# The up product of twelve MLP blocks by Strassen's scheme, in two rounds

## The chip, the cores and the metric

The kernel runs on one core of a Trainium2 chip, and its time is the device time of that core in microseconds, the median of three runs. A core has five engines that work side by side, each on its own list of instructions in order: TensorE (PE, matmuls), VectorE (DVE), ScalarE (ACT), GpSimd (POOL) and SyncE (SP, which here only issues DMAs). An instruction waits until those of other engines that it names in its semaphores are through, and everything behind it on its engine waits too.

## The reference

Three parts in a row, in float32, for 8 batches of 576 tokens:

```
phi(x) = exp(+-(x @ w_phi - max|x @ w_phi|))                # 64 -> 128 features, both signs
x   = (phi(q) @ (phi(k)^T v)) / (phi(q) . sum phi(k))       # linear attention, 8 heads of 64
xn  = layernorm(x) * g
x   = x + relu(xn @ w_ch1) @ w_ch2                          # 512 -> 2048 -> 512
th  = x @ w_theta
y   = w_tok_r @ (x cos th) + w_tok_i @ (x sin th)           # 576 x 576, over tokens
u   = x + y
out = u + relu(u @ w_ch)                                    # 512 -> 512
```

## The kernel before

Every float32 product is three matmuls on numbers that are split in a high and a low part: `mm3` (L74 to L77) issues high x high, high x low and low x high. A high part is a copy by ACT (`hi_act`), a low part the difference to it by DVE (`lo_vec`, L63) or POOL (`lo_pool`, L66). The big weights arrive as 64-bit numbers. `conv64` makes float32 of them with one ACT operation (L106) and four on DVE (L107, L108, L109, L114); `split64` adds the high and low parts.

The 2048 hidden units of the MLP are 16 blocks of 128. **Stage A** (up to 686 us) is attention, LayerNorm and the first 4 blocks for chunks of 256 tokens (`mlp_a`); after attention its last chunks remain, a tail from about 612 to 686 us, beside which the weights of the other 12 blocks are converted (`mb.loads`, at the lowest priority). Stage A leaves the normalised tokens in DRAM (`xn_d`) and the partial result (`xp_d`). **Stage B** (686 to 1312 us) does the other 12 blocks: 18 chunks of 256 tokens, each in six steps of two blocks. A step is `up` (24 `ph` matmuls of 256 columns), `relu` (L174 ACT, L175 DVE, with 512 columns each), and the `down` of the step before (12 `acc` matmuls of 512 columns). After the sixth step `flush_b` adds the partial result (L614) and stores the tokens (`x2_d`). The weights of the mixing are converted by `loads_mix` beside the first chunks, low parts on DVE. **Stage C** (1312 us to the end) takes batch after batch: `prep` loads and transposes a tile of 128 tokens, `theta` multiplies by w_theta and forms cosine and sine with POOL (L717), DVE (L718 to L720, L727, L63) and ACT (L723 to L725); `mix` and `channels` are the two products that follow. For the first batch, `prep` and `theta` are called inside the last chunk of stage B.

The order of the instructions on each engine is made once, when the program is built: a scheduler takes the calls with a priority (program order, moved down by `tc.high_priority(offset=LOWP)` or up by `HIP`) and lists them by its own estimate of when each can start.

Of the kernel before, what the change touches and what calls it, by code (L numbers as in the profile page):

```python
# [20 lines left out]
P = 128  # L21
# [30 lines left out]
def body(ctx, tc, qT, kT, va, wbd, g, w1, w2, wth, wtok, wch, out):  # L52
# [77 lines left out]
    class Mlp:  # L130
        """A range of the hidden units: weights and their loads, cut in steps of two blocks of 128."""
# [46 lines left out]
    # ---- attention and the first hidden units  # L178
# [393 lines left out]
    cur = tokens_b(0)  # L572
# [34 lines left out]
    def flush_b():
        acc, f, hh, hl, ch = pend
        mb.down(f, acc, hh, hl)
        if f == NFB // 2 - 1:  # L610
            x = p_mb.tile([P, CT, DM], F32, name="x")
            SY.dma_start(out=x, in_=xp_d[ch])
            for i in range(CT):
                V.tensor_tensor(x[:, i, :], acc[i], x[:, i, :], op=ALU.add)  # L614
            SY.dma_start(out=x2_d[ch], in_=x)

    # ---- rotation and the mixing of tokens and of channels: small tiles take the places of weights that are through
    class Slots:
        """Tiles that rotate through the slots of other tiles."""

        def __init__(self, *names):
            self.names, self.n = names, 0

        def tile(self, shape, dtype):
            tag = self.names[self.n % len(self.names)]
# [297 lines left out]
```

## Time and profile before

| what | us |
| --- | --- |
| median of three runs | 1757.18 (1756.98 to 1759.02) |
| span of the profiled execution | 1755.6 |
| median less span | 1.6 |
| stage B, 108 steps | about 686 to 1312 |
| stage C | about 1312 to 1755.6 |

The span is from the first to the last instruction of one profiled execution; what lies around it is the 1.6 us. Read the busy shares by stretch, not over the whole: DVE and POOL are loaded up to 740 us and again from 1312 us, while PE is loaded all the time.

```
PE   7899999899999898999999999999999999999999
DVE  8988798987898599886112212211247656656562
POOL 6786777777776243200000000000023222322220
```

These are tenths of busy time in 40 slices of 43.9 us each, from the page's second section; stage B is the slices 16 to 30.

### The profile page before, as it was taken

What the parts mean: (1) busy time and instruction counts of PE and PEld (TensorE: products, weight loads), DVE (VectorE), ACT (ScalarE), POOL (GpSimd) and SP (SyncE); (2) the same over time, 40 slices, a digit from 0 to 9 for tenths busy, and PEclk for the clock granted to TensorE, in tenths of its full rate; (3) what the DMA queues carried; (4) which work ended last, traced back from release to release, by engine and by line L of the source; (5) the groups of instructions that cost most, each with busy time, mean ns of one, the idle gap of its engine ahead of it and who ended that gap; (6) DMA issues with size and microseconds to landing.
All of it is one profiled execution on the core that took longest, in us unless ns stands there. A gap on an engine that the chain in (4) does not pass through costs nothing.

```text
span 1755.6 us, 29078 instructions
## 1 busy us (share of the span) xinstructions
PE 1691.7 (96%) x11596; PEld 1546.8 (88%) x11596; DVE 1076.5 (61%) x1910; ACT 670.5 (38%) x1236; POOL 601.4 (34%) x544
## 2 busy tenths in 40 slices
PE   7899999899999898999999999999999999999999
PEld 5787998899899687889999998999888999999999
DVE  8988798987898599886112212211247656656562
ACT  6675666666666434343111111111133223322330
POOL 6786777777776243200000000000023222322220
PEclk9999999999999999999999999999999999999999
DMA  5334333234331366445111111111032211212101
GB/s 182 98 101 125 92 111 111 79 104 127 103 113 58 120 197 192 155 138 176 49 37 49 61 37 37 64 46 37 25 98 77 70 52 38 57 46 75 52 14 41
DMA packets 80070, 151.13 MB, mean 86 GB/s; under 512 B 7232, under 2 KB 34240, under 8 KB 79936
## 3 DMA queue, kind: packets, MB, share of 16 engines
q1 hardware_dynamic: 79936, 149.29, 27.1%
q8 instruction: 91, 1.49, 0.4%
q14 instruction: 43, 0.35, 0.1%
HBM read 95.78 MB, written 49.28 MB: 83 GB/s over the span
## 4 chain that ended last, share of the span: by engine, by line
PE 76%; DVE 14%; POOL 3%; issue 3%; ACT 2%; DMA 1%; SPq 0%; DVEq 0%; POOLq 0%; ACTq 0%
PE ph L75 6%; PE ph L76 6%; PE ph L77 6%; PE acc L77 6%; PE acc L75 6%; PE acc L76 6%; PE mx L75 4%; PE mx L76 4%; PE mx L77 4%; PE ch L77 2%; PE ch L76 2%; PE ch L75 2%; PE th L76 2%; PE th L77 2%; PE th L75 2%
## 5 line engine op out<-in xcount | busy, mean ns | idle before, releaser
L175 DVE SCALAR_TENSOR_TENSOR hl<-ph,hh 128x512 fp32r<-128x512 f32 x138 | 95.0, 688 | 362.4 <-ACT hh L174 362.2
L75 PE MATMUL ph<-xh,w 128*128 128x256 f32 x1104 | 312.7, 283 | 2.6 <-DVE xl L63 1.6
L76 PE MATMUL ph<-xl,w 128*128 128x256 f32 x1104 | 311.4, 282 | 1.7 <-DVE xl L63 1.6
L77 PE MATMUL ph<-xh,w 128*128 128x256 f32 x1104 | 310.5, 282 | 0.0
L174 ACT ACTIVATE hh<-ph 128x512 fp32r<-128x512 f32 x138 | 82.0, 596 | 436.2 <-PE ph L77 426.0
L75 PE MATMUL acc<-w,hh 128*128 128x512 f32 x576 | 229.4, 399 | 4.8 <-ACT hh L174 3.1
L77 PE MATMUL acc<-w,hl 128*128 128x512 f32 x576 | 224.8, 399 | 3.5 <-DVE hl L175 3.4
L76 PE MATMUL acc<-w,hh 128*128 128x512 f32 x576 | 228.0, 396 | 0.0
L75 PEld LDWEIGHTS ph<-xh,w 128*128 128x128 f32 x1104 | 209.1, 189 | 9.4 <-DVE xl L63 1.6
L76 PEld LDWEIGHTS ph<-xl,w 128*128 128x128 f32 x1104 | 209.3, 190 | 7.8 <-DVE xl L63 2.5
L77 PEld LDWEIGHTS ph<-xh,w 128*128 128x128 f32 x1104 | 209.2, 190 | 0.3
L737 POOL TENSOR_TENSOR xs<-xs 128x512 f32<-128x512 f32 x4 | 5.5, 1374 | 560.5 <-DVE xs L63 560.5
L75 PE MATMUL mx<-wtk,xs 128*128 128x288 f32 x576 | 171.6, 299 | 1.3 <-POOL xs L57 1.3
L76 PE MATMUL mx<-wtk,xs 128*128 128x288 f32 x576 | 169.5, 295 | 0.0
L77 PE MATMUL mx<-wtk,xs 128*128 128x288 f32 x576 | 168.2, 295 | 0.0
L77 PEld LDWEIGHTS acc<-w,hl 128*128 128x128 f32 x576 | 106.6, 188 | 28.9 <-DVE hl L175 5.9
L75 PEld LDWEIGHTS acc<-w,hh 128*128 128x128 f32 x576 | 108.6, 189 | 25.1 <-ACT hh L174 3.9
L76 PEld LDWEIGHTS acc<-w,hh 128*128 128x128 f32 x576 | 108.4, 188 | 18.8
L270 DVE TENSOR_TENSOR ys<-pj,m 128x512 f32<-128x512 f32 (+1 forms) x160 | 99.6, 626 | 34.5 <-ACT pf L280 20.6
L75 PEld LDWEIGHTS mx<-wtk,xs 128*128 128x128 f32 x576 | 109.0, 189 | 2.0 <-POOL xs L57 1.8
L76 PEld LDWEIGHTS mx<-wtk,xs 128*128 128x128 f32 x576 | 109.1, 189 | 0.1
L77 PEld LDWEIGHTS mx<-wtk,xs 128*128 128x128 f32 x576 | 108.4, 189 | 0.0
(176 smaller groups left out, 4260.3 us busy)
## 6 DMA issues: line engine op xcount, KB each, us to landing
raw<-in_w SPq DMA_DIRECT2D x32, 512.0 KB, 3.8
in<-in_va SPq DMA_DIRECT2D x30, 325.0 KB, 3.0
xd<-xo SPq DMA_DIRECT2D x48, 192.0 KB, 2.1
x<-xd SPq DMA_DIRECT2D x36, 256.0 KB, 2.8
xnd<-xt SPq DMA_DIRECT2D x18, 512.0 KB, 3.0
xpd<-x SPq DMA_DIRECT2D x36, 256.0 KB, 2.9
xt<-xnd SPq DMA_DIRECT2D x18, 512.0 KB, 3.5
x<-xpd SPq DMA_DIRECT2D x18, 512.0 KB, 3.5
```

The source lines that it names most:

```text
L75: T.matmul(out_, lhsT=lh, rhs=rh, start=start, stop=False, **kw)
L76: T.matmul(out_, lhsT=lh, rhs=rl, start=False, stop=False, **kw)
L77: T.matmul(out_, lhsT=ll, rhs=rh, start=False, stop=stop, **kw)
L174: A.activation(hh, ph, AF.Relu)
L175: V.scalar_tensor_tensor(hl, ph, 0.0, f32(hh), op0=ALU.max, op1=ALU.subtract)
L270: V.tensor_tensor(ys[:, :2 * n, :], pv, m[:, :2 * n].unsqueeze(2).to_broadcast([P, 2 * n, NF]), op=ALU.subtract)
L737: G.tensor_tensor(x4, f32(pre[1]), f32(pre[2]), op=ALU.add)
```

## The change

Stage B works on 9 chunks of 512 tokens, in **two rounds** of three pairs of hidden blocks (54 steps, class `Hidden`). The up product of a pair is a 2 x 2 product of blocks: two halves of the 512 tokens by two halves of the 512 inputs (`a11`, `a12`, `a21`, `a22`), by two halves of the inputs by two hidden blocks. It is formed in seven parts instead of eight, in Winograd's form of Strassen's scheme, with four sums of token blocks (`s1` to `s4`, on POOL) and four of weight blocks (`tw`, on POOL). Each part is 6 matmuls of 256 columns (`part`), so a pair takes 42 instead of 48; results are combined on the way out of PSUM: some parts accumulate in one PSUM tile (`pa`), `keep` copies it on ACT, `plus` adds another on DVE, `relu` splits the sum (ACT and DVE, 256 columns). The down product is as before.

Round one leaves its partial sums in DRAM (`xq_d`). The weights of round two are prepared within round one (`loads_b`): two of the three pairs go to DRAM and come back by DMA at the end of the round, the third takes a free slot. The low parts of all these weights are made by POOL. The mixing weights are converted in round two (`loads_mix`), low parts on POOL; the token matrix now goes through DRAM (`wtk_d`). `prep` and `theta` of the first batch stand behind stage B.

```diff
+        def prep(self, stage, lo=lo_pool):
+            vs = stage.tile([P, KC, 2 * P], F32, name="vs")
+            for l in range(2):
+                val = self.conv(stage, w1[:, 2 * l:2 * l + 2, o:o + 2 * P], 2, 2 * P)
+                for c in range(2):
+                    A.activation(vs[:, 2 * l + c, :], val[:, c * 2 * P:(c + 1) * 2 * P], AF.Copy,
+                                 scale=gs[:, 2 * l + c:2 * l + c + 1])
+                yield
...
+            G.tensor_tensor(t[:, 0], b12, b11, op=ALU.subtract)
+            G.tensor_tensor(t[:, 2], b22, b12, op=ALU.subtract)
+            G.tensor_tensor(t[:, 1], b22, t[:, 0], op=ALU.subtract)
+            G.tensor_tensor(t[:, 3], b21, t[:, 1], op=ALU.subtract)
...
+            for d in (slice(3, 5), slice(5, 7)):
+                x = t[:, d.start - 3:d.stop - 3]
+                hi_act(h[:, d], x)
+                lo(l[:, d], x, h[:, d])
...
-        xt = p_m0.tile([P, KC, NC_], F32, name="xt")
-        SY.dma_start(out=xt, in_=xn_d[ch])
-        hi_act(xh, xt)
-        lo_vec(xl, xt, xh)
...
+        G.tensor_tensor(s1, a21, a22, op=ALU.add)
+        G.tensor_tensor(s2, s1, a11, op=ALU.subtract)
+        G.tensor_tensor(s3, a11, a21, op=ALU.subtract)
+        G.tensor_tensor(s4, a12, s2, op=ALU.subtract)
+        for n, src in (("a11", a11), ("a12", a12), ("s2", s2), ("s1", s1), ("s3", s3), ("a22", a22), ("s4", s4)):
+            h, l = (p_xb.tile([P, 2, NC_], F32R, name=n + i) for i in "hl")
+            hi_act(h, src)
+            lo_vec(l, src, h)
...
-            split64(p_st, wth[:, c, :], *wths[c])
+            split64(p_st, wth[:, c, :], wths[c][:, 0, :], wths[c][:, 1, :], pool_lo=True)
...
+        def part(self, ps, w, x, start, stop):
+            xh, xl = self.xs[x]
+            for k in range(2):
+                mm3(ps, self.q.wa[:, 0, w, k, :], self.q.wa[:, 1, w, k, :], xh[:, k, :], xl[:, k, :],
+                    start and k == 0, stop and k == 1, skip_group_check=True)
...
+        def first(self):
+            self.part(a, 0, "a11", True, True)
+            p1 = self.keep(a, "p1")
+            self.part(b, 1, "a12", True, True)
+            c11 = self.plus(b, p1, "c11")
+            self.relu(c11, 0, 0)
+            self.part(a, 4, "s2", False, True)
+            self.u2 = self.keep(a, "u2")
+            self.part(c, 3, "s1", True, True)
+            self.part(a, 5, "s3", False, True)
+            u3 = self.keep(a, "u3")
+            c22 = self.plus(c, u3, "c22")
+            self.relu(c22, 1, 1)
+        def second(self):
+            self.part(self.a, 6, "a22", False, True)
+            self.relu(self.a, 1, 0)
+            self.part(self.c, 2, "s4", False, True)
+            c12 = self.plus(self.c, self.u2, "c12")
+            self.relu(c12, 0, 1)
...
+    for r in range(2):
+        for ch in range(NCH // 2):
+            for n in range(NR):
+                hid = Hidden(slots[n], xs)
+                hid.first()
+                if pend is not None:
+                    flush_b()
+                hid.second()
+                if n == NR - 1 and not (r and last):
+                    cur = tokens_b(0 if last else ch + 1)
+                with tc.high_priority(offset=LOWP):
+                    next(gl if r == 0 else gx, None)
...
-                elif f >= 4:
-                    bs[0].theta(f - 4)
-                    bs[0].prep(f - 3)
...
+    x4, pre = shared_prep(0)
+    shared(0, pre)
+    for i in range(4):
+        bs[0].prep(i)
+        bs[0].keep(i)
+        bs[0].theta(i)
```

Three places show how the lists of instructions change. Lines are those of the kernel that the list belongs to.

PE within a step of stage B. Before, the end of an up product and what follows (`ph` is the PSUM tile of the up product, `acc` that of the down product, `w` a weight):

```order
L75 MATMUL ph<-xh,w_4_1_0_8269 128x256
L76 MATMUL ph<-xl,w_4_1_0_8269 128x256
L77 MATMUL ph<-xh,w_4_1_1_8270 128x256
L75 MATMUL acc_14205<-w_4_4_0_8281,hh 128x512 [waits Activation_49]
L76 MATMUL acc_14205<-w_4_4_1_8282,hh 128x512
L77 MATMUL acc_14205<-w_4_4_0_8281,hl 128x512 [waits DVE_49]
L75 MATMUL acc_14206<-w_4_4_0_8281,hh 128x512
```

The changed kernel, at the same place in a step (`pa`, `pb`, `pc` are PSUM tiles of the parts, `wa` and `wd` the weights of a pair):

```order
L75 MATMUL pc<-s4h,wa_8268 128x256
L76 MATMUL pc<-s4l,wa_8268 128x256
L77 MATMUL pc<-s4h,wa_8268 128x256
L75 MATMUL acc_9396<-wd_8269,hh 128x512 [waits Activation_49]
L76 MATMUL acc_9396<-wd_8269,hh 128x512
L75 MATMUL acc_9397<-wd_8269,hh 128x512
L76 MATMUL acc_9397<-wd_8269,hh 128x512
L75 MATMUL pc<-s1h,wa_8270 128x256 [waits DVE_49]
```

Before, the down product waits for one ReLU over both blocks, with the whole up product of the next step in front of it. Now `acc` takes the halves as they come, with a single part between a half's own product and its use, and the next part (`s1`) waits for DVE to have emptied `pc`.

DVE beside the conversion of weights. Before, in the first steps of stage B (`hl` is an eviction, `bits` and `val` the conversion, `xl` the tokens of the next chunk):

```order
L109 SCALAR_TENSOR_TENSOR bits<-raw,bits 128x512 [waits DVE_49]
L175 SCALAR_TENSOR_TENSOR hl<-ph,hh 128x512 [waits Activation_49]
L114 SCALAR_TENSOR_TENSOR val<-mag,bits 128x512 [waits DVE_49,Pool_49]
L175 SCALAR_TENSOR_TENSOR hl<-ph,hh 128x512 [waits Activation_49]
L63 TENSOR_TENSOR xl<-xt,xh 128x1024 [waits DMAHW2_49,Activation_49]
L107 TENSOR_SCALAR bits<-raw 128x512 [waits DMAHW0_49,DVE_49]
L175 SCALAR_TENSOR_TENSOR hl<-ph,hh 128x512 [waits PE_49,Activation_49]
```

The changed kernel, round one (`c` is a sum of parts on the way out of PSUM, `hl` the low part of its ReLU, `s3l` a token low part):

```order
L696 TENSOR_TENSOR c_9975<-pc,u_9973 128x256 [waits Activation_49]
L63 TENSOR_TENSOR s3l<-s_10026,s3h 128x512 [waits PE_49,Activation_49]
L117 SCALAR_TENSOR_TENSOR val<-mag,bits 128x512 [waits DVE_49]
L703 SCALAR_TENSOR_TENSOR hl<-c_9975,hh 128x256 [waits Activation_49]
L696 TENSOR_TENSOR c_10095<-pb,p_10087 128x256 [waits Activation_49]
L110 TENSOR_SCALAR bits<-raw 128x512 [waits DMAHW2_49,DVE_49]
L111 SCALAR_TENSOR_TENSOR bits<-raw,bits 128x512 [waits DVE_49]
L703 SCALAR_TENSOR_TENSOR hl<-c_10095,hh 128x256 [waits PE_49,Activation_49]
L112 SCALAR_TENSOR_TENSOR bits<-raw,bits 128x512 [waits DVE_49]
L703 SCALAR_TENSOR_TENSOR hl<-pa,hh 128x256 [waits Activation_49]
```

The conversion keeps its place between the evictions. There are now seven of those to a step, each half as wide, and the low parts of the weights are gone from the list.

PE at the end of stage B. Before, theta of the first batch in the last chunk (`th` theta, `tp` a transposed tile):

```order
L75 MATMUL acc_14206<-w_4_5_0_8283,hh 128x512
L76 MATMUL acc_14206<-w_4_5_1_8284,hh 128x512
L77 MATMUL acc_14206<-w_4_5_0_8283,hl 128x512
L75 MATMUL th<-wth_9472,xs 128x512 [waits Activation_49]
L76 MATMUL th<-wth_9473,xs 128x512
L77 MATMUL th<-wth_9472,xs 128x512 [waits DVE_49]
```

The changed kernel (`xs` here holds w_theta):

```order
L75 MATMUL acc_15403<-wd_12477,hh 128x512
L76 MATMUL acc_15403<-wd_12477,hh 128x512
L77 MATMUL acc_15402<-wd_12477,hl 128x512 [waits DVE_49]
L77 MATMUL acc_15403<-wd_12477,hl 128x512
L75 MATMUL th<-xs,xh 128x512 [waits Activation_49]
L76 MATMUL th<-xs,xh 128x512 [waits Pool_49]
L77 MATMUL th<-xs,xl 128x512 [waits DVE_49]
```

The last down matmuls come first now, all of theta behind them; its second and third rows wait for the low parts that POOL and DVE make.

## Rows read from the trace of the kernel before

**Rows 1.** The page, section 1: busy us (share of the span) and instructions of each engine.

```profile
PE 1691.7 (96%) x11596; PEld 1546.8 (88%) x11596; DVE 1076.5 (61%) x1910; ACT 670.5 (38%) x1236; POOL 601.4 (34%) x544
```

**Rows 2.** Stretches; columns: start:end, length, busy us (instructions) of each engine, PE's clock, DMA share, GB/s.

```profile
612.00:687.00 75.00, 68.25 (x423) 59.01 (x423) 73.73 (x101) 29.27 (x53) 28.69 (x19) 1.00 0.59 186
687.00:740.00 53.00, 48.33 (x307) 43.09 (x306) 46.71 (x62) 21.63 (x36) 13.70 (x9) 0.97 0.52 161
740.00:800.00 60.00, 60.00 (x376) 53.88 (x375) 52.66 (x117) 24.70 (x53) 0.00 (x0) 1.00 0.52 158
800.00:1200.00 400.00, 400.00 (x2547) 361.12 (x2547) 92.92 (x130) 59.57 (x94) 0.00 (x0) 1.00 0.17 56
...
1312.00:1350.00 38.00, 36.70 (x234) 33.21 (x233) 32.28 (x52) 15.39 (x28) 17.20 (x20) 1.00 0.32 110
```

**Rows 3.** PE's instructions in stage B; columns: start us, us, engine, line, operation.

```profile
901.29 0.39 PE L75 MATMUL acc<-w,hh 128*128 128x512 f32 x1
...
904.08 0.28 PE L75 MATMUL ph<-xh,w 128*128 128x256 f32 x1
...
906.95 0.39 PE L75 MATMUL acc<-w,hh 128*128 128x512 f32 x1
```

**Rows 4.** ScalarE and DVE around the same place.

```profile
901.49 0.60 ACT L174 ACTIVATE hh<-ph 128x512 fp32r<-128x512 f32 x1 [5.07 <-PE ph L77]
902.11 0.69 DVE L175 SCALAR_TENSOR_TENSOR hl<-ph,hh 128x512 fp32r<-128x512 f32 x1 [2.81 <-ACT hh L174]
```

**Rows 5.** DVE's operations by shape, 740 to 1200; after the bar busy us, mean ns.

```profile
L108 DVE SCALAR_TENSOR_TENSOR bits<-raw,bits 128x288 int32<-128x288 int32 x18 | 8.2, 455 | 0.4
...
L109 DVE SCALAR_TENSOR_TENSOR bits<-raw,bits 128x512 int32<-128x512 int32 x7 | 4.8, 687 | 0.1
...
L107 DVE TENSOR_SCALAR bits<-raw 128x512 int32<-128x512 int32 x6 | 2.6, 427 | 1.5 <-DMA raw<-in_wch 1.1 <-DMA raw<-in_wth 0.3
```

**Rows 6.** DVE's instructions at 692.

```profile
692.49 1.67 DVE L109 SCALAR_TENSOR_TENSOR bits<-raw,bits 128x512 int32<-128x512 int32 x1
```

**Rows 7.** POOL's instructions at 692.

```profile
692.01 1.60 POOL L66 TENSOR_TENSOR w<-val,w 128x512 fp32r<-128x512 f32 x1 [2.49 <-ACT w L120]
```

**Rows 8.** DVE's operations by shape, 612 to 740.

```profile
L109 DVE SCALAR_TENSOR_TENSOR bits<-raw,bits 128x512 int32<-128x512 int32 x25 | 24.7, 990 | 0.5
L108 DVE SCALAR_TENSOR_TENSOR bits<-raw,bits 128x512 int32<-128x512 int32 x26 | 23.2, 893 | 0.6
L114 DVE SCALAR_TENSOR_TENSOR val<-mag,bits 128x512 f32<-128x512 f32 x25 | 21.4, 856 | 1.3
L107 DVE TENSOR_SCALAR bits<-raw 128x512 int32<-128x512 int32 x26 | 14.8, 569 | 1.4 <-DMA raw<-in_wth 0.9
L175 DVE SCALAR_TENSOR_TENSOR hl<-ph,hh 128x512 fp32r<-128x512 f32 x13 | 8.8, 681 | 0.2 <-ACT hh L174 0.2
...
L481 DVE TENSOR_SCALAR xn<-x,lmv,lrs 128x512 f32<-128x512 f32 x8 | 6.6, 826 | 0.0
```

**Rows 9.** POOL's operations by shape, 612 to 740.

```profile
L66 POOL TENSOR_TENSOR w<-val,w 128x512 fp32r<-128x512 f32 x18 | 28.1, 1561 | 53.2 <-ACT w L120 34.2 <-ACT w L124 19.0
L489 POOL TENSOR_TENSOR xt<-xh,xl 128x512 f32<-128x512 f32 x10 | 14.4, 1445 | 33.9 <-DVE xl L63 25.5 <-PE tr L485 4.3 <-issue 3.5
```

**Rows 10.** The page, section 6: DMA issues, count, KB each, median us to landing.

```profile
xt<-xnd SPq DMA_DIRECT2D x18, 512.0 KB, 3.5
```

**Rows 11.** DVE's L720, once per tile of theta, at the start of the mixing.

```profile
1314.04 0.41 DVE L720 TENSOR_SCALAR xs<-xs 128x512 f32<-128x512 f32 x1
...
1321.72 0.43 DVE L720 TENSOR_SCALAR xs<-xs 128x512 f32<-128x512 f32 x1
```

**Rows 12.** A stretch of 2 us, columns as in rows 2.

```profile
724.00:726.00 2.00, 2.00 (x6) 1.60 (x5) 2.00 (x2) 0.47 (x2) 2.00 (x1) 0.50 0.06 16
```

**Rows 13.** PE's instructions around it; in brackets the wait and its releaser.

```profile
720.88 0.50 PE L75 MATMUL acc<-w,hh 128*128 128x512 f32 x1 [2.10 <-ACT hh L174]
...
726.08 0.36 PE L75 MATMUL ph<-xh,w 128*128 128x256 f32 x1
```

More of the change, by code (lines that the diff above doesn't have):

```diff
@@ L95, in body, with conv64 @@
     V.memset(halfpi, math.pi / 2)
-    def conv64(stage, src, pool_end):
+    def conv64(stage, src, pool_end, loaded=False):
         rows, n = src.shape
-        raw = stage.tile([rows, n], I64, name="raw", bufs=2)
-        SY.dma_start(out=raw, in_=src)
+        if loaded:
+            raw = src
+        else:
+            raw = stage.tile([rows, n], I64, name="raw", bufs=RAWB)
+            SY.dma_start(out=raw, in_=src)
         w = raw.bitcast(I32).rearrange("p (n two) -> p n two", two=2)
@@ L564, in body @@
+    NPR = NFB // 2
+    NR = NPR // 2
     s_st, p_st = opened(name="st1", bufs=1, side="right")
-    mb = Mlp(p_wb, p_st, NFA, NFB)
-    gl = mb.loads(*TAILM)
+    spare = Pair(NR + 1, NR)
+    slots = [Pair(m, m) for m in range(NR)]
+    gl = (None for q in slots for _ in q.prep(p_st))
     tail = chunk + 1
@@ new lines, in flush_b @@
+    def flush_b():
+        hid, acc, r, ch, n = pend
+        hid.down(acc, n == 0, n == NR - 1)
+        if n == NR - 1:
+            x = p_mb.tile([P, 2 * CT, DM], F32, name="x")
+            if r == 0:
+                for i in range(2):
+                    SY.dma_start(out=x[:, i * CT:(i + 1) * CT, :], in_=xp_d[2 * ch + i])
+            else:
+                SY.dma_start(out=x, in_=xq_d[ch])
+            for i in range(2 * CT):
+                V.tensor_tensor(x[:, i, :], acc[i], x[:, i, :], op=ALU.add)
+            if r == 0:
+                SY.dma_start(out=xq_d[ch], in_=x)
+            else:
+                for i in range(2):
+                    SY.dma_start(out=x2_d[2 * ch + i], in_=x[:, i * CT:(i + 1) * CT, :])
@@ new lines, in body, with loads_b @@
+    wx_d = [(dram.tile([P, 2, 7, 2, P], F32, name=f"wad{i}"), dram.tile([P, 2, 2, DM], F32, name=f"wdd{i}"))
+            for i in range(NR - 1)]
+    nxt_slots = []
+    def loads_b():
+        for i in range(NR - 1):
+            q = Pair(NR + 1 + i, NR) if i else spare
+            yield from q.prep(p_st)
+            SY.dma_start(out=wx_d[i][0], in_=f32(q.wa))
+            SY.dma_start(out=wx_d[i][1], in_=f32(q.wd))
+        q = Pair(NR, NR)
+        nxt_slots.append(q)
+        yield from q.prep(p_st)
@@ new lines, in body @@
+    flush_b()
+    for _ in gx:
+        pass
+    s_ps.close()
+    s_mb.close()
+    s_st.close()
+    s_xb.close()
+    s_p1, s_ps = ExitStack(), ExitStack()
+    ps_tr, ps_th = pool("xtp", 1, s_p1), pool("xth", 2, s_p1)
+    ps_mx, ps_ch = pool("xmx", 3), pool("xch", 2)
+    s_xc, pc = opened(name="xc", bufs=1, side="left")
+    wtks = [t[:, i] for q in slots for t in [in_slot("wa", q.slot, [3, 2, S])] for i in range(3)]
+    wtk_t = wtks
+    wchs = [t[:, i] for q in slots[:2] for t in [in_slot("wd", q.slot, [2, 2, DM])] for i in range(2)]
@@ L618, in body, with __init__, __call__ @@
+    wths = [(t[:, 0, :], t[:, 1, :]) for t in wths]
+    wtks = [(t[:, 0, :], t[:, 1, :]) for t in wtks]
+    s_xm, pm = opened(name="xm", bufs=1, side="left")
     class Slots:
[L621 to L625, printed above, removed]
+        def __init__(self, *places):
+            self.places, self.n = places, 0
+        def __call__(self, shape, dtype):
+            pl, tag = self.places[self.n % len(self.places)]
@@ L638, in body, with rot @@
+    def rot(pl, name, n):
+        return lambda shape, dtype: pl.tile(shape, dtype, name=name, bufs=n)
+    sl_z = Slots((p_wb, f"wd{slots[2].slot}"), *((pm, f"z{i}") for i in range(5)))
+    sl_x, sl_xh, sl_xl = rot(pc, "x", 3), rot(pc, "xh", 2), rot(pc, "xl", 2)
+    sl_k, sl_x4, sl_sc = rot(pc, "k", 3), rot(pc, "x4", 1), rot(pc, "sc", 4)
+    sl_cz = [rot(pm, "czh", 3), rot(pm, "czl", 3)]
     class Batch:
@@ L696, in prep @@
     def prep(p, t):
-        x = sl_x.tile([P, DM], F32)
+        x = sl_x([P, DM], F32)
         gt = p * NT + t
@@ L734, in shared_prep @@
     def shared_prep(p):
[L735 removed]
+        x4 = sl_x4([P, KC, P], F32)
         pre = prep(p, 4)
```

213 lines of the change are left out of this document (118 added, 95 removed).

## The prediction

> **What bounds the kernel now.** I read the page's busy line first: TensorE (PE) works 1691.7 us of a span of 1755.6, VectorE (DVE) 1076.5 [rows 1]. The table of stretches then says where that share is an average over two kinds of stage [rows 2]. From 612 to 740, the tail of stage A and the first steps of stage B, PE lacks 6.75 us of 75 and 4.67 of 53, and DVE is at 73.73 of 75. From 740 on PE has no gap: 60.00 of 60 while DVE still converts weights at 52.66 of 60 with GpSimd (POOL) idle, and 400.00 of 400 while DVE works 92.92. So in stage B only PE's own work sets the time, and its price can be read off the list of PE's instructions [rows 3]: 12 down matmuls of 512 columns take from 901.29 to 904.08, 2.79 us, or .2325 each; 24 up matmuls of 256 columns from 904.08 to 906.95, 2.87 us, or .1195 each; a step is 5.66. The eviction of a step is far from late: ReLU starts at 901.49 and the low part ends at 902.80 [rows 4], and its product is next needed 4 us later. A cut of PE's work in stage B is therefore worth its full length, as long as DVE and POOL keep up. That is the question here.
>
> **What the change removes.** A pair of hidden blocks over 512 tokens takes 48 up matmuls before, 42 after, all of 256 columns with a 128x128 weight as before; the down matmuls stay 24. There are 9 chunks of 512 tokens and 6 pairs, 54 in all: 54 x 6 x .1195 = -38.7 us. PE's part per pair becomes 42 x .1195 + 24 x .2325 = 10.6 us (11.3 before).
>
> **What it adds on DVE and POOL.** A conversion is four DVE operations; at 512 columns they take .43 + 3 x .69 alone [rows 5], 2.3 us from start to start with the small overlap that the rows show. Per pair, DVE gets seven evictions of 256 columns in place of two of 512 (about .35 each, an estimate at half of .69), and per chunk seven low parts of 512 (.60). That alone fits under PE. What doesn't is the neighbourhood of POOL. While a POOL subtraction runs from 692.01 to 693.61, a DVE operation on SBUF that began inside it takes 1.67 instead of .69 [rows 6, 7]. Grouped over 612 to 740: the conversion's L109, L108, L114, L107 take 990, 893, 856, 569 ns apiece, against 687 (L109, and the other two are of its kind) and 427 (L107) later, with POOL idle [rows 5, 8]. Over their 25 or 26 instructions that is 7.6 + 5.3 + 4.2 + 3.7 = 20.8 us, and 8 normalisations (L481) at 826, where an operation of this kind takes 427, add 3.2: 24 us for 28 POOL operations (18 and 10) [rows 8, 9]. So each costs DVE about .9 us. An eviction from PSUM isn't held: L175 takes 681 in the same stretch. [...]
>
> *Tail of stage A.* 12 conversions instead of 14 (-4.6 on DVE), but all 15 POOL operations of 512 and 15 of 256 of the first three pairs in place of 9 of 512: 6 x .9 + 15 x .45 = 12. DVE was at 73.73 of 75, so the 7 us more would show in full, less what the scheduler shifts: +3, bounds -5 (DVE stops being late at all, 6.75 back in part) to +7.
>
> *Start of stage B.* Nothing is left to convert there at once, but the first chunk's tokens pass a longer chain: the load xt<-xnd takes 3.5 [rows 10], then POOL makes s1 and s2 one after the other (3 us) and ScalarE and DVE split them (1.3), while PE has only the parts on a11 and a12, 1.4 us. I take about 8 us of idle, contention and slow clock against the 4.67 + .03 x 53 = 6.3 that stood there [rows 2]: +2, bounds -4 to +8.
>
> *Round one, its first seven pairs.* The order of the changed kernel has 14.7 conversions, 14 token low parts, 43 evictions and 8 sums of partial results there: 14.7 x 2.3 + 14 x .6 + 43 x .35 + 8 x .6 = 62 us of DVE, with 15 POOL operations of 512, 15 of 256 and 4 token sums: 19 x .9 + 15 x .45 = 24. That makes 86 us against 7 x 10.6 = 74 of PE, 12 too much. Since evictions from PSUM aren't held, I take 10. Bounds: 0, as in the row where 52.66 of 60 on DVE cost PE nothing, and 20, where each POOL operation holds DVE for its own 1.56.
>
> *Round two, its first eight pairs.* 18 conversions of 288 columns (.3 + 3 x .40 = 1.5 each, by the 455 ns of rows 5), 5 of 512, 18 token low parts, 57 evictions, 11 sums: 27 + 11.5 + 10.8 + 20 + 6.6 = 76. On POOL 18 low parts of 288 (at .5), 8 of 512 and about 12 token sums, of which I count 8: 9 + 14 = 23. That is 99 against 85 of PE, 14 too much; for the same reason I take 12, bounds 0 and 20.
>
> *All other pairs.* The seven evictions are in line with PE; one is tight: between the last part of a22 and the first acc matmul that needs its ReLU stand six matmuls of s4, .72 us, and ReLU needs .3 to .4 at 256 columns (half of the .60 in rows 4, plus its fixed part) and the hand-over: +2, bounds 0 to +8. Storing and reloading round two's weights and the partial sums finds the DMA engines at 17% in 800 to 1200 [rows 2]; I put that at 0, to +2.
>
> *Start of the mixing.* Before, theta of the first batch lies among the last chunk's matmuls, and PE lacks only 1.3 of 38 at 1312 [rows 2]. Now it stands behind stage B. After the last down matmul PE has five theta products of 2.8, transposes of about 2, and 7/9 of three mx groups of 27 (63 x .135 = 8.5): 24.5 us. They end on z of the fourth tile. That comes about 10 us for the first tile (theta 2.8, ScalarE, POOL, three DVE operations, sine, product, high and low part) plus four times DVE's work on a tile, nine operations or 5.1 us without POOL and 7.7 as it stands at 1314 to 1322 [rows 11]: 30 to 41, at 6.1 34.5. PE idles 10 instead of 1.3: +9, bounds +5 to +15.
>
> **Sum**, against the profiled execution: -38.7 + 3 + 2 + 10 + 12 + 2 + 9 = -0.7, a span of 1754.9. The median of the runs stands 1.6 above that span (1757.2 to 1755.6), so 1756.5 us: no change that shows. What can be told from no change is about .2%, 3.5 us.
>
> **Rivals.**
> First, DVE never gets late. For it: PE lost nothing in 740 to 800 with DVE at 88% [rows 2]; conversions are the lowest in priority. Against it: POOL was idle there, and POOL is what the change loads. Then each stretch costs 3 and the mixing 5: -38.7 + 3 + 2 + 3 + 3 + 2 + 5 = -20.7, 1736.5 us.
>
> [...]
>
> Third, the change doesn't do what it says: the seven parts, with their results evicted one by one through four PSUM tiles, never run at the pace of [rows 3]; .5 us of wait in every pair (the tight ReLU above with a late DVE) is 54 x .5 = 27, less the 2 already counted: 1781 us. Against it: the order puts 5 us of other matmuls in front of most uses.
>
> **How the numbers follow.** The forecast has .43, the first rival .29, the clock .22, the slow parts .06. The forecast's own range is 1747 to 1766, from half of the spread of its bounds; about .38 of it lies below 1753.7, .40 within 3.5 us of 1757.2, .22 above. Faster: .43 x .38 + .29 x .97 = .44. Same: .43 x .40 + .03 = .20. Slower: .43 x .22 + .22 x .95 + .06 = .36. The range that holds 8 in 10 runs from the first rival with its own spread to the second: 1733 to 1776.
>
> **What would show it.** Right: pairs of 10.6 us in the list of PE's instructions wherever no conversion stands beside them; in both conversion stretches DVE above 95% and PE with gaps that end on ACT hh, DVE hl or a DVE sum; DVE operations on SBUF of 1.3 us and more beside POOL subtractions; about 10 us of PE idle where theta starts, that ends on POOL or DVE. [...]

## The result

The changed kernel takes 1778.1 us (median of 4 runs, 1775.1 to 1779.4) against 1757.1 (1755.6 to 1759.0): ratio 1.0122, 95% interval 1.0107 to 1.0137. It is slower by 21 us, just above the range, where no change was forecast. Its profiled execution has a span of 1777.3.

The stretches of the changed kernel, with the columns of [rows 2]:

```profile
612.00:691.00 79.00, 70.54 (x414) 61.85 (x412) 70.80 (x87) 32.48 (x63) 54.68 (x40) 0.94 0.48 158
691.00:711.00 20.00, 15.98 (x84) 13.72 (x83) 14.08 (x21) 7.96 (x18) 12.11 (x8) 0.83 0.61 211
711.00:799.00 88.00, 70.20 (x402) 60.09 (x401) 85.31 (x119) 43.43 (x99) 49.64 (x38) 0.96 0.58 203
799.00:1008.00 209.00, 208.77 (x1307) 187.47 (x1307) 114.56 (x215) 78.72 (x189) 32.55 (x24) 1.00 0.35 127
1008.00:1144.00 136.00, 124.66 (x736) 108.33 (x735) 119.99 (x212) 61.60 (x151) 53.31 (x42) 0.97 0.61 204
1144.00:1305.00 161.00, 160.59 (x999) 143.82 (x998) 82.76 (x157) 56.68 (x137) 21.99 (x16) 1.00 0.33 117
1305.00:1380.00 75.00, 67.41 (x393) 58.34 (x392) 52.81 (x83) 27.58 (x50) 27.57 (x32) 0.98 0.31 98
```

A pair has 66 matmuls. From 799 to 1008 PE is full and does 1307 of them in 209 us, 10.55 us a pair: the saving is there. From 711 to 799 it does 402, or 6.1 pairs, in 88 us where 64.5 would do, and DVE is busy for 85.3 of them. From 1008 to 1144 it is 736, 11.2 pairs, in 136 where 118 would do.

To put every microsecond somewhere, I call *lost time* what has passed less what the matmuls begun until then take at full pace (.1192 for 256 columns, .2328 for 512, .1333 for 288); waits and slow clock both count. It grows as follows; the first two rows are set right under "Why the prediction was wrong".

| term | forecast | before | after | measured |
| --- | --- | --- | --- | --- |
| PE's work | -38.7 | 1717.0 | 1679.8 | -37.2 |
| lost until stage B begins | +3 | 24.8 | 28.9 | +4.1 |
| its start (before: to 740; after: one pair) | +2 | 7.2 | 8.5 | +1.3 |
| round one, pairs 2 to 7 | +10 | 0 | 23.8 | +23.8 |
| round two, pairs 1 to 11 | +12 | 0 | 17.8 | +17.8 |
| all other pairs | +2 | .4 | .8 | +.4 |
| start of the mixing, 66 us | +9 | 3.0 | 13.3 | +10.3 |
| the rest | 0 | 3.2 | 4.4 | +1.2 |
| span | -0.7 | 1755.6 | 1777.3 | +21.7 |

What PE waits for between 711 and 799 (engine, line, waited for: us in total, times, longest):

```profile
PE acc L77 <- DVE hl L703: 10.9, 5, 3.2
PE acc L75 <- ACT hh L702: 2.9, 3, 2.4
PE pb L75 <- DVE c L696: 2.2, 1, 2.2
PE pc L75 <- DVE c L696: 1.8, 1, 1.8
```

All of it is late evictions. DVE's operations there, by shape:

```profile
L111 DVE SCALAR_TENSOR_TENSOR bits<-raw,bits 128x512 int32<-128x512 int32 x14 | 17.5, 1247 | 0.3
L703 DVE SCALAR_TENSOR_TENSOR hl<-c,hh 128x256 fp32r<-128x256 f32 x18 | 13.6, 770 | 0.0
...
L110 DVE TENSOR_SCALAR bits<-raw 128x512 int32<-128x512 int32 x13 | 10.5, 805 | 0.1
...
L703 DVE SCALAR_TENSOR_TENSOR hl<-pa,hh 128x256 fp32r<-128x256 f32 x6 | 2.5, 411 | 0.0
```

The conversion is held by POOL as in [rows 8]: L111 takes 1247 ns on the mean where L109, the same kind of operation, takes 687 in [rows 5]; L110 takes 805 where L107 takes 427. Look at the two forms of L703, one and the same operation: with the sum in SBUF (`hl<-c`) it takes 770 ns, straight from PSUM (`hl<-pa`) 411. This is how one wait comes about; first DVE, then POOL, then PE:

```profile
745.20 1.77 DVE L112 SCALAR_TENSOR_TENSOR bits<-raw,bits 128x512 int32<-128x512 int32 x1
746.89 2.36 DVE L703 SCALAR_TENSOR_TENSOR hl<-c,hh 128x256 fp32r<-128x256 f32 x2
749.17 0.41 DVE L703 SCALAR_TENSOR_TENSOR hl<-pa,hh 128x256 fp32r<-128x256 f32 x1
```

```profile
745.12 2.44 POOL L66 TENSOR_TENSOR wa<-vs,wa 128x512 fp32r<-128x512 f32 x2
747.53 2.86 POOL L66 TENSOR_TENSOR wa<-tw,wa 128x512 fp32r<-128x512 f32 x2
```

```profile
749.63 0.73 PE L77 MATMUL acc<-wd,hl 128*128 128x512 f32 x2 [1.93 <-DVE hl L703]
```

Four POOL subtractions run back to back from 745.1 to 750.4. One conversion step and two evictions of .41 take 1.77 and 2.36 beside them. The eviction that PE waits for is the third one, `hl<-pa` from PSUM: it isn't held itself (.41), but DVE's list is in order, and PE stands 1.93 us until it is through at 749.58.

That POOL is the reason, and not the place of the operand alone, shows within one form: of the 18 `hl<-c` from 711 to 799, the nine with no POOL operation beside them took 409 to 414 ns, the nine others 1130 on the mean (411 to 1507). POOL's *hold* is a name for this lengthening; where an expectation below says lock, no more than this is measured.

### The profile page after: what moved, and what is told of

Same layout as the page of the kernel before. It is cut to its first block, busy times and chain, and to the rows that moved or that the text cites. A ratio compares the mean times of both kernels' runs of the same rounds, so it can differ in the third digit from the quotient of the medians.

```text
span 1777.3 us, 29747 instructions
## 1 busy us (share of the span) xinstructions
PE 1677.1 (94%) x11272; PEld 1524.4 (86%) x11272; DVE 1286.8 (72%) x2292; ACT 805.4 (45%) x1644; POOL 781.8 (44%) x684
## 4 chain that ended last, share of the span: by engine, by line
PE 67%; DVE 20%; issue 4%; POOL 4%; ACT 3%; DMA 2%; SPq 0%; DVEq 0%; POOLq 0%; ACTq 0%
PE acc L77 5%; PE acc L75 5%; PE acc L76 5%; PE mx L75 4%; PE mx L76 4%; PE mx L77 4%; PE pa L76 2%; PE pa L77 2%; PE pa L75 2%; DVE bits L111 2%; PE ch L77 2%; PE ch L75 2%; PE ch L76 2%; DVE bits L112 2%; DVE hl L703 2%
## 5 line engine op out<-in xcount | busy, mean ns | idle before, releaser
L75 PE MATMUL acc<-wd,hh 128*128 128x512 f32 x432 | 173.5, 402 | 7.2 <-ACT hh L702 4.2
L77 PE MATMUL acc<-wd,hl 128*128 128x512 f32 x432 | 163.7, 401 | 16.2 <-DVE hl L703 16.2
L76 PE MATMUL acc<-wd,hh 128*128 128x512 f32 x432 | 172.6, 400 | 0.0
L75 PE MATMUL mx<-xs 128*128 128x288 f32 x512 | 151.1, 296 | 0.5 <-POOL xs L57 0.4
L76 PE MATMUL mx<-xs 128*128 128x288 f32 x512 | 151.2, 296 | 0.0
L77 PE MATMUL mx<-xs 128*128 128x288 f32 x512 | 149.4, 296 | 0.0
L703 DVE SCALAR_TENSOR_TENSOR hl<-c,hh 128x256 fp32r<-128x256 f32 x162 | 101.1, 630 | 22.6 <-ACT hh L702 22.4
L271 DVE TENSOR_REDUCE m<-pj 128x4 f32<-128x512 f32 (+1 forms) x160 | 98.6, 622 | 13.7 <-PE pj L77 13.1
L66 POOL TENSOR_TENSOR kpl<-pf,kph 128x512 fp32r<-128x512 f32 (+1 forms) x75 | 96.2, 1283 | 19.4 <-ACT kph L60 16.8
L75 PEld LDWEIGHTS acc<-wd,hh 128*128 128x128 f32 x432 | 82.9, 192 | 21.3 <-ACT hh L702 5.2
L283 ACT ACTIVATE pf<-ys 128x512 f32<-128x512 f32 (+1 forms) x160 | 85.5, 586 | 34.0 <-DVE ys L273 13.3
L75 PEld LDWEIGHTS mx<-xs 128*128 128x128 f32 x512 | 96.2, 188 | 1.4 <-POOL xs L57 1.2
L696 DVE TENSOR_TENSOR c<-pc,u 128x256 f32<-128x256 f32 x108 | 44.9, 416 | 71.9 <-ACT u L691 71.7
L76 PEld LDWEIGHTS mx<-xs 128*128 128x128 f32 x512 | 96.2, 188 | 0.0
L77 PEld LDWEIGHTS mx<-xs 128*128 128x128 f32 x512 | 95.6, 188 | 0.1
L76 PE MATMUL kv<-kpl,vh 128*65 128x256 f32 x300 | 87.9, 293 | 6.2 <-DVE kpl L63 6.0
```

The costliest lines, as they stand in the source:

```text
L66: G.tensor_tensor(dst, src, f32(hi), op=ALU.subtract)
L75: T.matmul(out_, lhsT=lh, rhs=rh, start=start, stop=False, **kw)
L76: T.matmul(out_, lhsT=lh, rhs=rl, start=False, stop=False, **kw)
L77: T.matmul(out_, lhsT=ll, rhs=rh, start=False, stop=stop, **kw)
L271: V.tensor_reduce(m[:, :2 * n], pv, axis=AX.X, op=ALU.max, apply_absolute_value=True)
L283: A.activation(kp[:, :2 * n, s, :], ys[:, :2 * n, :], AF.Exp, scale=sc)
```

## The experiments

All times are medians; ratios are to the kernel before on the same chip. *R1* is the lost time from the second pair to the end of round one, *R2* that of round two, *M* that of the 70 us at the start of the mixing. Theory: in the crowded pairs DVE has more to do than PE, by its conversions and by POOL's hold on it. Rivals stand with each run. R1, R2 and M come from one profiled execution of each kernel, which lies between 1.4 us below its median and 3.3 above.

| run | us | ratio, 95% interval | R1 | R2 | M |
| --- | --- | --- | --- | --- | --- |
| changed kernel | 1778.1 | 1.0122 (1.0107 to 1.0137) | 24.1 | 18.1 | 13.3 |
| e1, no conversion | 1762.6 | 1.0046 (1.0031 to 1.0061) | 9.3 | 17.4 | 13.4 |
| e2, no POOL | 1762.9 | 1.0048 (1.0033 to 1.0063) | 9.1 | 17.9 | 13.5 |
| e3, low parts on DVE | 1757.5 | 1.0013 (1.0002 to 1.0023) | 10.3 | 9.8 | 14.5 |
| e4, loads held back | 1802.1 | 1.0265 (1.0249 to 1.0280) | 16.6 | 32.8 | 29.2 |
| e5, paced, low parts on DVE | 1747.1 | 0.9947 (0.9931 to 0.9964) | 9.7 | 0 | 15.0 |
| e6, paced, low parts on POOL | 1743.4 | 0.9929 (0.9914 to 0.9944) | 3.6 | 3.7 | 13.1 |
| e7, e5 and a new start of the mixing | 1754.9 | 0.9993 (0.9983 to 1.0002) | 9.7 | .4 | 21.2 |
| e9, e6 with ScalarE at the start | 1742.2 | 0.9923 (0.9908 to 0.9937) | 2.4 | 4.1 | 14.1 |
| e10, e6 with two steps a pair | 1756.4 | 1.0008 (0.9997 to 1.0018) | 17.4 | 4.1 | 14.8 |
| e11, e6 with three | 1759.4 | 1.0014 (1.0005 to 1.0024) | 18.9 | 4.5 | 14.8 |
| e13, e10 without POOL's weight part | 1756.9 | 1.0001 (0.9992 to 1.0011) | 15.1 | 5.3 | 14.2 |
| e14, e10 with token sums on DVE | 1759.2 | 1.0017 (1.0008 to 1.0027) | 9.8 | 12.4 | 15.4 |
| e15, e6 with token sums on DVE | 1757.1 | 1.0002 (0.9992 to 1.0011) | 10.0 | 11.8 | 15.3 |
| e16, e9 with mixing low parts on DVE | 1737.8 | 0.9889 (0.9872 to 0.9905) | 2.4 | 1.2 | 11.9 |

**e1 and e2: half of DVE's burden taken away, in two ways.** In round two's weights (`m >= NR`):

```diff
+        if skip:                      # e1
+            A.activation(val, hi32.bitcast(F32), AF.Abs)
+            return val
...
+                lo = lambda dst, x, hi: A.activation(dst, x, AF.Copy)     # e2
+                for i, x in enumerate((b12, b11, b22, b21)):
+                    A.activation(t[:, i], x, AF.Copy)
```

> Left out: the four DVE operations of each conversion for the weights of round two (12 conversions, done within round one); their value is replaced by the magnitude that ScalarE makes, so these weights are wrong. Loads, POOL's sums and low parts, and everything else stay. Theory (in the first six pairs after the start of stage B, DVE has 86 us of work beside 64 us of PE): DVE loses about 28 us, falls under PE, and 18 to 21 of the 23 us that PE waits between 711 and 799 us come back: 1758 us. Rival A (POOL's chain of sums and low parts, 54 us, or the raw loads hold evictions back whatever DVE has to do): at most 6 us come back: 1772 or more.

> Left out: POOL's part in the weights of round two (12 sums and 18 low parts, 38 us of POOL between 711 and 799 us); ScalarE copies stand in their place, so these weights are wrong. All conversions on DVE stay. Theory: DVE's operations return to the durations that they have with POOL idle, 22 us less on DVE, and 15 to 20 of the 23 us come back: 1760 us. Rival B (the conversions and evictions alone are too much for DVE, or ScalarE, which gets 30 operations or 17 us more, becomes late): at most 8 us come back: 1770 or more.

Each brought back 15 us of R1 (18 to 21 were expected of e1), and nothing elsewhere. So most of the loss, 15 of 24 us, needs both: the conversions, and POOL beside them. Rivals A and B fall. In e1 8 of the 9 us that stay lie between 743 and 771, beside conversions of w_theta, which this run keeps. Its longest wait there, 3.65 us, stands behind six POOL operations in a row, four of them the token sums, with three conversion operations on DVE. In e2 what stays is spread over seven pairs, about 2 us at most in one; its cause wasn't tried.

**e3: low parts back on DVE.** `lo = lo_pool if self.m < NR else lo_vec`, and `pool_lo=True` dropped three times.

> The low parts of round two's weights and of the mixing weights are made by DVE, as those of the mixing weights were in the kernel before, instead of POOL; the four sums of weight blocks stay on POOL. Theory (a POOL subtraction costs DVE .7 us, about what the operation costs DVE itself): round one gains 12 us on DVE by 18 fewer POOL operations and loses 10, round two gains 14 and loses 12: 1774 us, between 1768 and 1780. Rival C (POOL takes load off DVE as the change intends): DVE gets 22 us more in two places where it is the bound: 1795 or more.

By the ratios 19 us came back, 22 by R1 and R2, where I expected 4. The direction says that POOL relieves nobody here, and rival C falls; the size is more than the balance of DVE explains.

**e4, e5, e6: the same work, spread.** e4 holds back the load of each conversion, e5 and e6 its first DVE operation. e4 takes one step of the mixing weights to a pair, e5 and e6 two in two pairs of three:

```diff
+        if hold:      # e5, e6; hold[-1] is the ReLU of the pair in whose place this is written
+            A.activation(bits.bitcast(F32)[:, 0:1], f32(hold[-1][:, 1, 0:1]), AF.Copy)
...
                 with tc.high_priority(offset=LOWP):
                     next(gl if r == 0 else gx, None)
+                    if r and n != 1:
+                        next(gx, None)
```

> The same work, spread: every raw load of the weights of round two and of the mixing waits for a one-element ScalarE copy that reads the ReLU of the pair in whose place the load is written, so that the scheduler cannot move conversions ahead to the first pairs: one step of the loads to a pair. Theory (DVE is the bound only where conversions are crowded): with one conversion to a pair DVE needs about 9 us of 10.6, and the 23 us of round one and the 13 to 17 us of round two fall to some 3 each: 1748 us, between 1742 and 1756, faster than both kernels. Rival A (it is POOL's chain or the waits for single operations): each conversion still delays its pair, 1770 or more.

> Low parts on DVE as in the run before that did so, and the conversions paced in another way than by their loads: loads run ahead freely, but DVE's first operation of a conversion waits for a one-element ScalarE copy that reads the ReLU of the pair in whose place the conversion is written; in round two, two pairs of three take two steps of the mixing weights, so that they are through after 16 pairs. Theory (what was lost when the loads were held back was DVE standing behind late loads, 42 us of waits; what is lost without pacing is DVE overfilled): round one's 10 us and round two's 10 us fall to 3 each: 1744 us, between 1738 and 1752. Rival D (any conversion beside a pair delays its evictions, however spaced): 1757 or more.

> The same pacing with the low parts on POOL as in the changed kernel. Theory (DVE has room once the conversions are spaced, even with .7 us for each POOL operation: 9.5 us of 10.6): round one 23 to 5, round two 18 to 6: 1748 us, between 1742 and 1760. Rival E (the lock matters wherever a POOL subtraction stands, since the evictions that it delays are near their deadlines): 1765 or more.

e4 came out at 1802 where 1748 was expected. DVE's waits there, 690 to 1330, and PE's for an eviction, 700 to 1330:

```profile
DVE bits L117 <- DMA raw<-in_wtok: 26.6, 12, 2.7
...
DVE bits L117 <- DMA raw<-in_wth: 10.4, 3, 4.2
```

```profile
PE acc L77 <- DVE hl L711: 29.4, 14, 3.1
```

DVE's list is in order: a conversion whose load is late holds the evictions behind it. But that is not all. The nine longest of these 14 waits, 25 of the 29.4 us, all stand behind the four token sums of a chunk on POOL with conversion operations on DVE beside them, and while eight of them also have a late load before them (1.0 to 2.5 us), the first, 2.71 us to 777.29, has none. What each of the two costs wasn't tried. Two conversions are also left over for the start of the mixing, where e4 has an M of 29.2.

With the loads free and the operation held (e6), the place that lost 24 us loses 3.6, with the same work on the same engines and a one-element ScalarE copy to each conversion:

```profile
711.00:895.00 184.00, 182.62 (x1135) 163.27 (x1134) 133.63 (x228) 85.38 (x214) 60.43 (x49) 1.00 0.43 151
895.00:990.00 95.00, 94.28 (x585) 84.01 (x584) 54.12 (x97) 35.76 (x86) 18.41 (x13) 1.00 0.46 166
990.00:1110.00 120.00, 118.70 (x735) 105.80 (x734) 101.51 (x189) 56.23 (x153) 38.82 (x33) 1.00 0.52 180
1110.00:1270.00 160.00, 158.54 (x985) 141.89 (x984) 102.25 (x190) 64.20 (x162) 32.19 (x25) 1.00 0.45 160
1270.00:1350.00 80.00, 72.85 (x422) 62.33 (x421) 54.80 (x87) 28.29 (x51) 29.08 (x33) 0.98 0.30 97
```

PE is at 182.6 of 184 us, DVE at 133.6. Rivals A, D and E fall: what costs is the crowd. e5 came near its time, but not by its theory: R1 stayed at 9.7 where 3 was expected, and R2 fell to 0. And here low parts on POOL win in round one (3.6 against 9.7) and lose in round two (3.7 against 0).

**e7 and e9: the start of the mixing.** For the first batch `hi_act` in place of `hi_pool` on z, and `A.activation(dst, tp, AF.Copy)` in place of POOL's `keep`; e7 also gave the token tiles a fourth place (`tag="u1"`).

> As the paced kernel with low parts on DVE, and the start of the mixing rebuilt for the first batch: the high parts of z and the transposed tokens by ScalarE straight from PSUM instead of POOL, and a fourth place for the token tiles, so that the third tile's load need not wait. Theory (the start of the mixing is bound by DVE's work on a tile, lengthened by POOL, and by one late load of 2.9 us): PE's 14 us of waits and slow clock there fall to 8: 6 us below the paced kernel, 1738 us. Rival F (the chain of one tile sets it, whatever the engine): within 2 us of the paced kernel.

> The paced kernel (low parts on POOL) with the start of the mixing rebuilt in one point only: for the first batch, high parts of z and the transposed tokens come from ScalarE instead of POOL; no extra place for a token tile, whose load cost the last run of this kind 8.7 us. Theory (POOL's operations lengthen DVE's there): 3 to 6 us below the paced kernel, 1739 us. Rival F (the chain of one tile sets it): within 2 us of 1743.

e7's load into the extra place was issued only at 1283.59, when the last matmul of stage B had begun (1281.70), and PE stood for it. That stage B held the memory until then is the likely reason, not shown:

```profile
PE tp L919 <- DMA xf<-x2d: 8.7, 1, 8.7
```

Without it (e9) the kernel is within 1.2 us of e6, less than its interval, and that difference lies in R1, which the edit doesn't touch. Rival F's bound holds: the work that POOL gives up here is not what sets the time. That the chain of a tile sets it is what remains, and isn't shown.

**e10 and e11: how crowded is too crowded.** `for _ in range(1 or 2): next(gl, None)` more per pair in round one.

> The paced kernel with two steps of the loads to a pair in round one instead of one: 12 conversions in 9 pairs, 1.33 to a pair. By the balance of DVE (4.6 us a pair of its own and .9 for POOL's token sums; 2.3 a conversion and 1.4 for the POOL operations that belong to it) DVE needs 10.4 us of 10.6: round one loses some 3 us more than in the paced kernel, 1746 us, between 1743 and 1750. Rival G (what pacing cures is not DVE's load but the order within a pair): 1743, no difference.

> Three steps of the loads to a pair in round one: 12 conversions in 6 pairs, 2 to a pair, as crowded as in the changed kernel but held to their pairs. By the same balance DVE needs 12.9 us of 10.6 in six pairs, 14 us more than PE: 1757 us, between 1752 and 1764. Rival G: 1743 to 1747.

e11 came out as expected, e10 didn't: 14 us lost more than in e6, with DVE at 79 of 103 us in its crowded pairs:

```profile
742.00:845.00 103.00, 93.93 (x545) 82.75 (x544) 79.05 (x122) 47.06 (x117) 37.99 (x31) 0.93 0.45 160
```

A mean load doesn't tell, and since e11 was worked out from the same balance, its hit is luck. Rival G's 1743 came in neither. Of e10's 17.4 us some 6 are slow clock: by this row's granted .93, (1 - .93) x 93.9 = 6.6. The place in e10 where PE waits longest, DVE, POOL, PE:

```profile
811.52 1.52 DVE L707 SCALAR_TENSOR_TENSOR hl<-c,hh 128x256 fp32r<-128x256 f32 x1
812.96 1.77 DVE L115 SCALAR_TENSOR_TENSOR bits<-raw,bits 128x512 int32<-128x512 int32 x1
814.65 1.48 DVE L707 SCALAR_TENSOR_TENSOR hl<-c,hh 128x256 fp32r<-128x256 f32 x1
816.05 1.75 DVE L63 TENSOR_TENSOR a12l<-xt,a12h 128x512 fp32r<-128x512 f32 x1
```

```profile
810.01 1.30 POOL L637 TENSOR_TENSOR s<-xt 128x512 f32<-128x512 f32 x1 [7.50 <-DMA xt<-xnd]
811.28 1.48 POOL L639 TENSOR_TENSOR s<-xt 128x512 f32<-128x512 f32 x1
812.71 1.47 POOL L66 TENSOR_TENSOR wd<-val,wd 128x512 fp32r<-128x512 f32 x1
814.14 1.71 POOL L638 TENSOR_TENSOR s<-s,xt 128x512 f32<-128x512 f32 x1
815.92 1.33 POOL L640 TENSOR_TENSOR s<-xt,s 128x512 f32<-128x512 f32 x1
```

```profile
818.19 1.22 PE L77 MATMUL acc<-wd,hl 128*128 128x512 f32 x2 [3.52 <-DVE hl L707]
```

Five POOL operations in a row; DVE gets one operation through for each of them, two of them evictions of .41. PE's wait again ends on the `hl<-pa` behind them.

**e13, e14, e15: who makes the runs of POOL operations.** e13 is e2's edit in e10; e14 and e15 put the four token sums on DVE (`V.tensor_tensor` for `G.tensor_tensor`) in e10 and e6.

> As the kernel with two steps to a pair, and left out: POOL's part in the weights of round two (sums and low parts; ScalarE copies instead, so these weights are wrong). The four token sums of a chunk stay on POOL. Theory H (PE waits where POOL runs operation behind operation, since then every DVE operation on SBUF, an eviction of .41 us too, takes as long as a POOL operation, 1.3 to 1.8 us): the token sums alone still make four in a row, but no fifth and no run of seven: about 9 of the 13 us come back, 1747 us. Rival G (the order of conversions among the evictions is to blame, not POOL): 1754 or more.

> As the kernel with two steps to a pair, but the four token sums of each chunk on DVE instead of POOL (2.4 us more on DVE in three pairs); POOL's part in the weights stays. DVE's load is the same within .1 us a pair, since the sums' .9 us of lock goes. Theory H: the runs of four and five POOL operations that the token sums make are gone, those of the weights stay: about half of the 13 us come back, 1750 us. Rival I (DVE's mean load decides): no change, 1756.

> The paced kernel, low parts on POOL, one step to a pair in round one, with the token sums on DVE. Theory H: 54 x 4/3 POOL operations fewer, and no eviction is held by them: the 3.6 us that round one and the 3.6 that round two still lose shrink to about 2 each, and the first chunk's chain of sums is shorter (.6 instead of 1.5 us an operation), 2 us: 1739 us. Rival I: 1743, no change.

Without POOL's part in the weights e10 gains 2 us of R1 at most (15.1), and 1756.9 us is in rival G's range. With the sums on DVE its R1 falls from 17.4 to 9.8, no more than e15 has with one step to a pair (10.0). So it is the four sums in a row beside conversions that cost it. The trace of e13 shows the place. PE's three long waits in its R1, 3.3, 3.4 and 2.9 us, all stand behind the four token sums, and POOL does nothing else there. DVE and PE at the second, where the sums run from 773.9 to 779.7:

```profile
773.97 1.74 DVE L115 SCALAR_TENSOR_TENSOR bits<-raw,bits 128x512 int32<-128x512 int32 x1
775.64 2.93 DVE L712 SCALAR_TENSOR_TENSOR hl<-c,hh 128x256 fp32r<-128x256 f32 x2
778.49 1.75 DVE L116 SCALAR_TENSOR_TENSOR bits<-raw,bits 128x512 int32<-128x512 int32 x1
780.16 0.68 DVE L63 TENSOR_TENSOR a12l<-xt,a12h 128x512 fp32r<-128x512 f32 x1
780.77 0.41 DVE L712 SCALAR_TENSOR_TENSOR hl<-pa,hh 128x256 fp32r<-128x256 f32 x1
```

```profile
781.23 0.73 PE L77 MATMUL acc<-wd,hl 128*128 128x512 f32 x2 [3.40 <-DVE hl L712]
```

The same four sums in e6, from 865.7 to 871.5, with no conversion beside them:

```profile
865.67 2.98 DVE L707 SCALAR_TENSOR_TENSOR hl<-c,hh 128x256 fp32r<-128x256 f32 x2
868.58 1.78 DVE L63 TENSOR_TENSOR a12l<-xt,a12h 128x512 fp32r<-128x512 f32 x1
870.28 0.41 DVE L707 SCALAR_TENSOR_TENSOR hl<-pa,hh 128x256 fp32r<-128x256 f32 x1
```

```profile
870.75 0.73 PE L77 MATMUL acc<-wd,hl 128*128 128x512 f32 x2 [0.76 <-DVE hl L707]
```

The two evictions are held in both, 1.5 us each. What e13 has besides are two conversion operations in front of `hl<-pa`, 3.5 us under POOL's hold. So theory H and rival G are each half right: the order puts conversions there, and POOL makes them long.

But the sums on DVE lose 1 us in nearly every chunk, also where nothing is converted, so that R2 triples and e14 and e15 end higher. Four sums and seven low parts in one go are a crowd too. My expectation for e15 was wrong in sign.

**e16: each place its better side.** Low parts of round two's weights on POOL, of the mixing weights on DVE.

> The paced kernel with ScalarE at the start of the mixing, low parts of round two's weights on POOL (round one), low parts of the mixing weights on DVE (round two). In the paced runs round one lost 3.6 us with low parts on POOL and 9.7 with them on DVE, round two 3.7 and 0. If the two places are independent: 3.5 us less than with POOL in both, 1739 us, between 1736 and 1742, and the best of all. If the order that the scheduler lists is what decides, and it changes all through with one edit: anything from 1739 to 1755.

1737.8 us, 1.1% faster than the kernel before and within the range expected if the two places are independent. Of the 4.4 us by which its median lies below that of e9, R2 has 2.9; M has 2.2, which the expectation didn't have. Round two, 988 to 1110, and the start of the mixing:

```profile
988.00:1110.00 122.00, 121.51 (x755) 108.48 (x754) 103.96 (x210) 57.39 (x157) 22.21 (x16) 1.00 0.54 181
1110.00:1270.00 160.00, 159.55 (x990) 142.95 (x989) 102.33 (x198) 63.55 (x160) 22.31 (x16) 1.00 0.47 164
1270.00:1345.00 75.00, 68.36 (x402) 59.16 (x401) 50.50 (x86) 36.09 (x65) 14.27 (x18) 0.98 0.29 91
```

## Why the prediction was wrong

- *PE's saving*, -38.7: right; pairs of 10.55 us where nothing else crowds. The pages count 11596 and 11272 matmuls, 324 fewer or 54 x 6, which is -38.6 at .1192. That the table has -37.2 is not PE's price: counted over all matmuls, the changed kernel had lost 1.9 us more by 612 us already, in stage A ahead of its tail. So the table's first two rows are rather -38.6 and about +5.5.
- *Tail and start of stage B*, +3 and +2: +4.1 and +1.3. The sizes are near, but the tail's by luck. The forecast had 7 us more work on DVE; DVE worked 70.80 of 79 us there, less than the 73.73 of 75 before, and PE's idle time grew from 6.75 to 8.46 only. What it hadn't counted is the clock, .94 where it had been 1.00: .06 x 70.54 = 4.2.
- *Round one*, +10: this step failed. DVE's work was sized well: 86 us forecast, 85.3 busy of 88. What I set against it was wrong: "7 x 10.6 = 74 of PE". The 43 evictions that I had counted belong to six pairs, at seven each, so that the same PE had 64 us, and DVE's excess is 22, not 12. Measured are 23.8. The balance is not the whole mechanism either: e10 loses 17.4 at 79 us of DVE in 103, and in round two a full DVE costs nothing for 30 us (below). What the runs show in its place is where the loss falls, at conversions and evictions that stand beside a run of POOL operations. A smaller slip hides beside it: I excused the evictions from POOL's hold as reading PSUM, but three of four `hl` of a pair read a sum in SBUF, and took .77 on the mean instead of .41, 6.5 us in that stretch. (One reading was off too: the five L481 with no POOL operation beside them took 534 ns, not 427, so the 24 us of hold read from [rows 8] are 23.)
- *Round two*, +12: 17.8. The sum was 14; I took 2 off for those evictions, and the first pairs meet the token sums and three low parts of w_theta in a row (one wait of 3 us for DVE's sum, to 1018). DVE is full from 1010 to 1097, as forecast, but most of that time PE loses nothing by it. In the second of these rows its loss follows the token sums, which run with three low parts of the weights from 1054.5 to 1063.4:

```profile
1026.00:1058.00 32.00, 31.83 (x199) 28.24 (x197) 31.32 (x66) 17.57 (x44) 9.86 (x10) 1.00 0.75 243
1058.00:1075.00 17.00, 13.85 (x71) 10.86 (x70) 16.56 (x32) 7.59 (x21) 8.14 (x8) 0.90 0.71 240
```

- *Other pairs*, +2: .4. The ReLU that I thought tight wasn't, outside the crowded pairs.
- *Start of the mixing*, +9: 10.3, right in size. DVE's L928 (L720 before) comes every 7.0 us there (5.7 to 8.1), between the 6.1 chosen and [rows 11]; e9 shows that the POOL operations that it replaces aren't the reason. What PE waited for came out otherwise: of 7.4 us of waits from 1305 to 1380, 3.1 end on ScalarE's `xh` and 2.9 on one load, which I hadn't seen, and only 1.4 on DVE or POOL.
- The rivals: the first and the third are refuted, DVE does get late (10.9 us of PE's waits from 711 to 799 end on its `hl`), and the parts do run at pace (10.55 us a pair from 799 to 1008). What the forecast calls the clock, at .22 and with 1776 at the upper end of its range, rests on a term that no run shows, a fixed loss behind a wait: [rows 12, 13] have a clock of .50 behind one wait of 2.10 us, not that the one follows from the other. What the runs show in its place is a share: (1 - clock) x PE's busy time, summed over the stretches above, is 14.7 us, 1.5 to 1.6 before [rows 2]: 4.2 in the tail, 2.7 at the start of stage B, 2.8 in round one, 3.7 in round two, 1.3 at the mixing. That 1776 lies near the measured 1778.1 is in good part luck: it is 19.5 us above the forecast, and a slow clock has 14.7 in all. Nor is it the cause in round one. From 711 to 799 DVE is full, so that PE would have waited at either clock (argued, not tried), and in e6, where the same pairs run at 1.00, what changed is the place of the conversions.

With six pairs in that one line (22 in place of 12, less the same 2) the forecast would have been about 1767, and its sign right; the other 11 us would still have been missing.

What stays open: how long a run of POOL operations an eviction can bear. Two cases are measured. Four token sums beside evictions and a token low part cost PE 0 to .8 us a time (e6, round one); with two conversion operations among them, 2.9 to 3.4 (e13). e10 loses at a mean DVE load little above that of e6, and I have no rule that would have told it in advance.

## What to carry to other kernels

When a stretch is bound by what stands beside it, count both sides in the same unit: seven evictions make a pair, so 43 make six. A scheduler that fills idle engines early crowds low-priority work into the first places it finds; pacing it by a dependency on the work beside it turned this loss of 1.2% into a gain of 0.7%, and choosing the engine for each place into 1.1%. Here the dependency had to be on the operation; on its load the kernel became slower by 24 us. What work moved to POOL cost differed by place: with the low parts on POOL round one lost 3.6 us and round two 3.7 (e6), with them on DVE 9.7 and 0 (e5). It was a matter of what stood beside each run of POOL operations, not of DVE's mean load: e10 lost 17.4 us in round one with DVE busy for 79 us of 103, e6 3.6 with 133.6 of 184.

## What was not expected of the hardware

- One DVE operation, L703, takes 411 ns with an operand in PSUM and 770 on the mean with both in SBUF: 411 with POOL idle, 1130 with POOL operations beside it. In e10, from 811 to 817 with POOL operations back to back, DVE passed one operation on SBUF for each, whether of 256 or 512 columns: 1.5 us for an eviction of .41, 1.75 for a low part of .69.
- The TENSOR_SCALAR L110, whose one input is in SBUF, is held too: 805 ns on the mean from 711 to 799, where L107 takes 427 in [rows 5]. L696, which adds an operand in SBUF to one in PSUM, isn't: 411 to 413 ns on the mean in the same stretch.
- Four sums moved from POOL to DVE (.69 us each in e15 where nothing holds them) cost about 1 us of PE a chunk, 2.8 us in the three of e15 from 861 to 959, even where DVE, in the changed kernel, is busy for 52 us of 100 (860 to 960).
